# One read for two PSUM banks, double buffers for exponentials, and a new order of work

## The chip, the cores and the metric

The kernel runs on one core of one Trainium2 chip. The metric is the device time of one execution in microseconds (us); the time before is the median of three runs. The profile is one execution, recorded by the hardware profiler. Its engines are PE (TensorE: matmuls), PEld (loads of weights into TensorE), DVE (VectorE), ACT (ScalarE), POOL (GpSimd) and SP (SyncE, which issues all transfers here).

## What is computed

Two branches read the same `x` (2048 tokens of 512) and are mixed by a gate for each token. One is attention with 32 heads of 16 that share one key and one value head, without a mask; the other a gated feed-forward layer of width 1792.

```python
def _A_ref(x, wq, wk, wv, wo):          # B 1, S 2048, D 512, H 32, Dh 16
    q = (x @ wq).reshape(B, S, H, Dh).transpose(0, 2, 1, 3)
    k = x @ wk
    v = x @ wv
    scores = jnp.einsum("bhqd,bkd->bhqk", q, k) * (Dh ** -0.5)
    p = _softmax(scores, axis=-1)
    o = jnp.einsum("bhqk,bkd->bhqd", p, v)
    return o.transpose(0, 2, 1, 3).reshape(B, S, H * Dh) @ wo

def _B_ref(x, w_gate, w_up, w_down):
    g = jnp.einsum("bsd,df->bsf", x, w_gate)
    u = jnp.einsum("bsd,df->bsf", x, w_up)
    return jnp.einsum("bsf,fd->bsd", _sigmoid(g) * u, w_down)

x = A_x
g = _sigmoid((x * gate_w).sum(-1, keepdims=True))
return g * _A_ref(x, A_wq, A_wk, A_wv, A_wo) + (1 - g) * _B_ref(x, B_w_gate, B_w_up, B_w_down)
```

## The kernel before

**Tiling.** Tokens come in 4 blocks of 512 (`NB`, `TB`), keys in 16 chunks of 128 (`NC`). A *unit* is one block of queries for four heads; there are 32 units (`NU`). Matmuls of the feed-forward layer, of the output projections, of the scores and of the maxima use half of the array's rows: the lower lane (h = 0) rows 0 to 63, the upper one (h = 1) rows 64 to 127. The two lanes run at the same time, each into a PSUM bank of its own. Precision is kept by splitting operands into a high and a low part (three products for one), so a projection is a long row of accumulating matmuls.

**The softmax of a unit.** First its maxima: 128 matmuls of queries by keys (line 1092), each into a bank that a reduce on DVE (line 1094) reads at once, 64 for each lane; `max_finish` and `max_turn` fold the partial maxima and SP writes them back into rows of the queries, so that the next matmuls come out less the maximum. Then the scores: 128 matmuls of keys by queries (line 1101), each into a bank that an `Exp` on ACT (line 1103) reads and writes to a buffer `p` in SBUF. Last the values: for each chunk of keys four matmuls over the whole array (line 977; the trace has eight records for them) take the four buffers of that chunk, and sixteen chunks accumulate in one bank. That bank is copied out by ACT (`finish`, line 984) whenever a run of value products ends, since the halves may use other banks next; parts of one unit are added on POOL (line 991). The sums of exponentials take the way over DRAM (`store`, `sums`, `invert`, `send_inverse`, `spread`) and POOL divides by them (`divide`).

**The order.** Nothing is left to a scheduler. `ORDER` is a text, one code for each slot of TensorE, and `plan()` walks it with a clock of its own (`State`). A hexadecimal digit is a slot of two half-array matmuls: the digit divided by 4 says what the lower lane does, the remainder what the upper lane does, 0 nothing, 1 a maximum, 2 a score, 3 a fill (one matmul of a feed-forward or output job). So `5` is a maximum in both lanes, `a` a score in both, `f` a fill in both, `7` a maximum below and a fill above. `V` is a value product, `T` the transpose of maxima, `G` a projection or a transpose of the first stage; these three use the whole array. A `.` is a pause: it moves the clock by 25 units and issues nothing. A slot moves it by 100 units, the change from whole array to halves by 94 (`OUT`) and back by 52 (`IN`).

The clock knows the queues: `on(engine, at, cost)` appends work to an engine. `RED = 260` units is a reduce, `EXP = 208` an exponential, `COPY = 210` a copy; a bank counts as free `TAIL + FREE` units after the computed end of a reduce (38 + 65) and `TAIL_A + FREE_A` after that of an exponential (52 + 60). `take()` gives the bank that has been free longest. `can_s` holds the scores back while all `PB = 21` buffers are in use. Tasks for POOL carry a rank, and an order of SP's transfers follows from the same clock. The result is a list of acts, written out as instructions; at the end of the program every engine is tied to exactly this order. On the chip the clock counts for nothing more: each instruction starts when its engine reaches it and its semaphores allow it.

**The first and the last microseconds.** The first stage (`G`) projects keys, values and queries; `first_x`, `keys_out` and `query_out` keep their tiles in the same ring of `p` buffers. At the end the output projection of the last block has its job in two parts: `a` (three of four head groups; nine fills for each lane and tile) and `e` (unit 30, three fills below only), whose weights `we` are split on POOL (lines 731 and 732) into a ring of four buffers `wd`. The last two heads' share follows from the last bank by transposes (lines 1128 to 1150).

Of the kernel before, what the change touches and what calls it, by code (L numbers as in the profile page):

```python
# [9 lines left out]
F32 = mybir.dt.float32  # L10
F32R = mybir.dt.float32r
AF = mybir.ActivationFunctionType
# [6 lines left out]
P = 128  # L19
# [11 lines left out]
RAW, WB, DB, PB, HB, BA_BUFS = 2, 2, 4, 21, 6, 4  # L31
# [13 lines left out]
EXP, COPY, SCALED = 208, 210, 247  # L45
TAIL, TAIL_A = 38, 52
# [65 lines left out]
class State:  # L112

    def __init__(self):
# [26 lines left out]
        self.held, self.exps = 0, []  # L141
# [329 lines left out]
    def can_s(self, h):  # L471
        j = self.ep[h]
        return (j < NU * NC * 2 and j < self.ep[1 - h] + H_LEAD and self.held < PB
                and self.max_ready.get(j // (2 * NC), NEVER) <= self.now)

    def issue_m(self, h):
        i = self.take()
        self.acts.append(("m", h, self.mp[h], i))
        self.mp[h] += 1
        self.free[i] = self.on("dve", self.now + LATE, RED) + TAIL + FREE  # L480
        if self.mp[h] == min(self.mp) and self.mp[h] % (2 * NC) == 0:
            u = self.mp[h] // (2 * NC) - 1
            self.acts.append(("max_finish", u))
            self.maxima.append((u, self.on("dve", 0, ENDS)))

    def issue_s(self, h):
# [17 lines left out]
    def issue_v(self):  # L504
# [7 lines left out]
        self.held -= 4  # L512
# [106 lines left out]
    def step(self, code):  # L619
# [10 lines left out]
        else:  # L630
# [15 lines left out]
    "GGGGGGG555G55G555.G551G554.G..G55G555G55GG555G55G5ff7ffddff7f5ffffff7fdff7ffdff5G55GTG555G577Gbfed9fedbf6fb7edeb"  # L646
    "7fbd6fdbfef6dbfb7edff55VVVVdaf7f6bdfe7bf9fedb7bed7efedef7bdb7bedff7f55VV555VVV7b7b7bb77bbfdedefedeedfedfedb7bb7b"
    "df6fddd7dVVVTV6ef7f6f9febdf6f9f6fbe7fbdf9e7fe7bf9dbf6ff5dVV695VV696V5bfef6f9fbdef6bdb7ff5dVV5a6.V969V7b6efdfe79f"
    "be7fe7bddd7VVTV5bfedeb7fbde7eb7efdf57VV6ddefbf9fe7bf9fe7b7f5dVVVde6edfb7f9fb7be7dbfe7bdbff6dedbf6fbe7bdfef5VV555"
    "VVV7b7b5bfefededb7ef9fedb7bff6edfed6fbbd7bffd5TVV565VVV5adffeb7fb7edbb7def6febdfe7f9bfdb7ee7edf9f7VV695VVV79fe7b"  # L650
    "def6fef97bfed6fbdbf7edbf9f6feb7dffd75VVa5aVV5a9VV6f7ef97efbd6fbb7efdf5eVV996Vde7bb7efdebde7fe7bdf5bVTV9a5V6de7fb"
    "f9f6fbf6f9fedf5bVV6edfb7f6fbdebdf6fbdf5bVVVV6dfbf67bfedbbdf6fed6fbf6fbdf6bfd9fef6fffb95VV656VV9a5VV5efbf79feb7ef"
    "d9fe7bedff6bfdb7ef9f6fbdb7fed5VTV65aVVVV5bfef97ef9f6febdfe7b7eedf7bbdefdb7be7efd7f6VV959VVV7bdef6dbfe7afdb7f9fed"
    "be7ef7f9bfd6fbf6dfff55VVa5aVTVVVde7bdbe7f9fef6bdbf7edb7bff6debfdb7eed7ef9f7VVde.de7b7bff56VV9dfb7bfedafaVVV6debf"
    "7f9faf9VV76bfede7fdb5VV7b7bbfdedee7e7fed9ff5bVV76bfdef6fbdbdeb7efdf67VV999V67fe7bfedbdeb7f9fe7fd6VTV5a6V5bfededb"
    "fb7ef6f9fdf577VVV97fedbdbfe7ef97bedfb7ee7fdb7befd9feb7fe7fd5VV696VV95aVV7bdef6f9fe79fbedef7e7bdbfedf6fbdaff6dfbf"
    "775VTVVVV97fef9bdf6f9fe7ebfd6feb7dfb7ebfd9feb7fbd7deV569VV65aVVV97fedb7efedb7bf6efde7bdbff6dbfb7edef6dbf7d7VVVVV"
    "9a7ffde7f9fee7dbbdf6fef97bfdbfe7afdfb67ffd6V969VTVa69VV6a6VV9fdbb7edf9fef6f9bf7ffbf7eedf9fe79fee7ff57VV599VVV6f7"
    "bdedbfe7af7debf7f9fffedbb7fed6fbedff75VV596VV9562VV95fefeb7f9faf7f6bfdf5eVV7b79febdfbdee77eedff5bVTV95aV6b7bfdb7"
    "fedef6f9bfde7dVV56aV9b77fedefbdbf6f6dbff6dVV9a5VV6b7ff9def6fbdb7e7ef9fedbfb7debf76fbdefdff55VVVVV6bb7fdfedbe7f6f"  # L660
    "9f6fbed7bff9fed6feb7bdf6ffd9V5a5VTVVV7a7fdebdfb7afd7efb7edbe7ff9f6defb7eedfb7df5VVVa95VVV7a7bfde7fedbbd7bef7eded"
    "bbf7e7fbde7edbbfd7edV5a5VV6b7ff9e7f9fef97ebfde7dVTV6a5Vadf7fbde7bf6f9fe79fd7eVVa95VV6a5Va7fdbf7edb7efbde7bddfaVV"
    "65aV9b7b7fedfe7bdee7fbdd7dVVVV7a7ff9e7fbdef9f6fe7bdbe7dbffe5efbedfb7fef55VVVa95VTVV6b7bfde7f9fef9f6f6f9fee7ff97b"
    "edf9fbf6fdff66VV996VV9a5VV6b7ff97efed6fbdbfb7edbdef7eed7bf9fe7bf7fdd5VVVVV6b7fedbdf6fbbdb7fe7edbef7debdfb7edbfe7"
    "e7f5eV996VTV699VVV7a7fbdf6fbdef9e7fb7bdef6fdbedfe79fbe7fd7ef5VVV977bfefedfa6VV9a9VV5a6V5bfbed7efbf77bb7VdedadedV"
    "V7b7bedfedaf6VV7b7beddefbe5fefb79fef5VV5edeede.f77f9fbbf7bf5faVTV5a6V9b7fdee7fbdaf7edf7fd79VV59aV6b7fdbfedb7af7d"
    "efdf75dVVV7b7bdedef6fbf9f6fbd6fef97efdbfe79fe7bfdff56VV9a5VTVV6b7fdbedf6fef9b7b7fedef97fbdefe79fee7fb7fd5VVV9a5V"
    "VV797bfee7fed9feb7f9fe7ebd7bfe7bdfb7edefedfb6VV965VV965VV97bbf7defe7afdf9ef7e7bdbff6dbf6fedbfe5bfed7TVVV9a5VVV7b"
    "5bb7fefedef6dbef7bdbbdf6f7ef9fede7bf7fde5VV695VV5a6V9b7bfde7fbdee7f9bfde7dVV7a7ff9edf6fe7bbdfee6f7VV959VV9f7eb7d"
    "efedbb7f6efdfedff6fbfb7bbdb7edfef5TVV9a6VV9a5VV6a5V97fbe7edfbdeb7ed7bff5dVV7bb7b7bdfededeb7ffdb77bfbfeedf6feedff"  # L670
    "57ddVVV6a5V977bfef9f6fafddefb75fdVVVV7a7dfbedfeb7be7dfafdb7f6fdefb7eeddbfb7eff95TVVVVV7b5bfee7fedbe7dbefdb7ee7ff"
    "9bdfb76fef9fbdef5V569VVVV6b7fdb7efbdaf7edf6fbdbf6bdf7efed9feb7f5fd7dVVVVV6b7bfde7f9fedeb77bfedbe7ff9efdb7e7ef9fb"
    "d6fdV5a5VV7a7bfde7f9fef9e7f9f7edTVVVVV7a7dfebdfe7bed7bfbdf6fffbedf6f9fe7bbd7fedVVVV7b6fdef9fe7bdbe7fbd6ff77bbVVV"
    "dedeedb7fe7ebddbf6fb7bedbfd7befd6ffee76VV955VTVV9b7fdbedfb7e7edbfedb7edb7eff6dbfbde7bfdff55VVVVV6b7fbdedf6fb7ede"
    "bfdb7ebd7fb7ebfdbdee7fffe65VV995VVV6b7ff9e7fedb7edbe7fedb7bf9fbdf6f6fbf6ffde5dVTVa95VVVV6b7fdeb7f9feed7bf6f9fb7e"
    "feddb7efedb7bfbde7dVV5a5VV6b7ff9edfbe5VV7a7fbdefdbe5VV6b7ff9edfaf5VV6b7bfdfedfa5V7be7fedbbde7f9fe7bdfffef6fb7bbd"
    "edfef67e.f5VV95aV97b7fedbfbde7eede7f7f9VTV95aV6b7bfdbdfe7ede7ebf7df5VVa95VVVV6b5ffbe7f9fe7bdeef79fe7bf9fe7fed9fe"
    "7bffdf66VV9a5VV9a5VV7b7edbf6f9fef9e7edfb7bfe7f97efedbfbd6ffe5f5VVVa95VVTV7b7bdee7f9fedb7bfe7edbf6dbfdee7f9feb7e7"
    "fef5V995VV5a5VVV7a7ff9e7fbde7eedfbdb7bf6edfbde7f6fbbdedf6f7VV995VVV6b7bfde7fbdafd7ef9f6fbdef7ede7bfb7edbff57deVT"
    "Va95VV7a7ff9e7f9fef97edefb7dVV6b7dfeb7f9fee7db7eff9dVVV7a7ff9e7fbdee7dbf9ff6dVV6b7ff9e7fedbf6f9fbdf6dVV6a9VTVVV7"  # L680
    "b79fe7efedaf7edef7dffefbb7bdf9fb7ee7ff9eV5a5VV969V7b7b97fefedee7defb75fdVV5b7bfef9f6feedfbdb7f5dVVVV7a7ff9e7fedb"
    "b7edfed6fbdbfe7edfb79fe7efffb55VVVa95VTVV7a7fdbe7f9febdb7fede7eb7fedb7f9fede7bf6ffd9V5a5VV6a9VVV6b7fdeb7fedbdeb7"
    "fedb7bedbf7dbfe7e7ef9f7d5fdVVVVV7a7bfde7f9fede7bf9f6fbb7dfeedfb7b7edefbd7deV695VV7a7bfdedfb7be7edef79fdVV6a5Vadf"
    "7fb79fef6fbdbd6fd7eVVa95VVTV7a5ffbedf6fbf6bdfe7f9fbfff6dbfedaf7d77fdeVVa95VVVV6b7ff9edf6fbf9b7fed6feb7feddbfe7e7"
    "bdbefffa5VTV595VVV7a7ff9e7fedb7ef9efdb7b7ef9ff6defb7bedfdff65VVa95VVVV6b7bfdedf6fbdeb7fbde7ee7dfbdbfe7b7bedfffe9"
    "5VV695VVV6b7dfebdf6fb7beddefe7bbd7fefb79fe7edefb7f5dVTVa95VVVV6b7fbde7f9fe7bededfb7be7dfe7bdefb7bdefbd6fdVV7b79f"
    "ebdfee5VV5efbe7bdfe7aVV9b7fbdfe7ed5VVV7b7bedefdafaVV6bff6bf9fb7fdef6fefaeVV9b7b7feef9f9ffdef6bfea.VVaaaVVVabbbbb"
    "VVTfeeefafeefbfffffffebaffefbffeVVaaVVVbbfeaVbeaVbaeVafffffbbfffefeeebbVVaefffbbbffeeefVabffffbefeffaVVaaaVVaaaV"
    "Vaa8VV..............Vcccccccccccc"
# [11 lines left out]
def tile_kernel(ctx, tc, x_in, wq, wkv, wo, wg, wu, wd, consts_in, out):  # L701
# [14 lines left out]
    banks = [pp.tile([P, 512], F32, tag=f"bank{i}", name=f"bank{i}") for i in range(8)]  # L716
# [20 lines left out]
    def first_x(b):  # L737

        XR[b] = [ap.tile([P, 512], F32, tag="p", name=f"xf{b}_{kc}", bufs=PB) for kc in range(KC)]
# [158 lines left out]
    def keys_out(b, _, ps):  # L898
        kh = ap.tile([P, TB], F32, tag="p", name=f"kh{b}", bufs=PB).bitcast(F32R)
# [3 lines left out]
        VT[b] = ap.tile([P, TB], F32, tag="p", name=f"vt{b}", bufs=PB)  # L903
# [24 lines left out]
    def query_out(b, t, ps):  # L928
        hi, lo = QD[b, t] = [ap.tile([P, TB], F32R, tag="p", name=f"q{b}_{t}_{i}", bufs=PB) for i in range(2)]
# [270 lines left out]
```

## Time and profile before

| | us |
|---|---|
| three runs | 1599.39, 1599.62, 1601.97 |
| median | 1599.62 |
| the profiled execution | 1598.83 |
| its span, first to last instruction | 1597.1 |

| 40 us from | PE | DVE | ACT |
|---|---|---|---|
| 0 | 37.66 | 28.17 | 18.84 |
| 80 | 40.00 | 38.97 | 27.65 |
| 1540 | 40.00 | 5.23 | 39.91 |

The granted TensorE clock is 1.0 throughout. The page's first lines give busy time and share of the span for each engine. Its costliest groups read: line, engine, operation, output and inputs, shape, count, then busy time and mean ns of one, then idle time of that engine just before them and what ended it. The chain of waits lists start, length and instruction, merged where neighbours are alike. A row of the windows view gives, after its bounds and its length, busy time with the count of instructions for PE, PEld, DVE, ACT and POOL, then the clock, the DMA share and GB/s.

### The profile page before, as it was taken

How to read it: one execution, taken by the hardware profiler on the slowest of the kernel's cores; microseconds unless marked ns; L12 is line 12 of the kernel's file. 1: busy time of each engine (PE TensorE's matmuls, PEld its weight loads, DVE VectorE, ACT ScalarE, POOL GpSimd, SP SyncE). 2: the span in 40 equal slices, each digit the busy share in tenths (PEclk: the TensorE clock that was granted, in tenths of full speed). 3: DMA queues.
4: the chain of work that ended last, by engine and by line, in shares of the span. 5: the costliest groups of instructions: out<-in, count | busy, mean ns of one | idle time of the engine just before them, and what ended most of it. 6: DMA issues, size and time to landing. Idle time of an engine off the chain costs nothing.

```text
span 1597.1 us, 33902 instructions
## 1 busy us (share of the span) xinstructions
PE 1587.9 (99%) x12918; PEld 998.6 (63%) x12918; DVE 1392.0 (87%) x2372; ACT 1258.4 (79%) x2474; POOL 848.0 (53%) x708
## 2 busy tenths in 40 slices
PE   9999999999999999999999999999999999999998
PEld 7776665665656566566666566666656665656654
DVE  7999998998988989988998898889989998988832
ACT  4268778888878878879878877878987887878896
POOL 4254364558363664375745446454936366536463
PEclk9999999999999999999999999999999999999999
DMA  7621121115111212013411121111502021201111
GB/s 239 216 80 42 42 57 36 45 59 137 29 68 32 75 56 60 18 39 83 111 37 58 39 75 54 55 38 59 137 28 68 32 75 46 71 16 42 34 36 44
DMA packets 54678, 102.31 MB, mean 64 GB/s; under 512 B 18232, under 2 KB 19768, under 8 KB 53492
## 3 DMA queue, kind: packets, MB, share of 16 engines
q1 hardware_dynamic: 54516, 100.16, 21.0%
q8 instruction: 101, 1.65, 0.4%
q14 instruction: 61, 0.50, 0.1%
HBM read 74.05 MB, written 13.09 MB: 55 GB/s over the span
## 4 chain that ended last, share of the span: by engine, by line
PE 98%; ACT 0%; DVE 0%; DMA 0%; POOL 0%; issue 0%; DVEq 0%
PE bank L1071 31%; PE bank L977 29%; PE bank L1092 18%; PE bank L1101 16%; PE bank L838 4%; ACT p L1103 0%; PE bank L963 0%; PE bank L908 0%; DVE ba L1148 0%; DVE ba L1034 0%; DMA wkv_raw<-wkv 0%; POOL wkv_s L732 0%; DVE wkv_stack L869 0%; PE bank L1144 0%; DVEq L1196 0%
## 5 line engine op out<-in xcount | busy, mean ns | idle before, releaser
L1094 DVE TENSOR_REDUCE mx<-bank 128x1 f32<-128x512 f32 x2048 | 1257.4, 681 | 133.8 <-PE bank L1092 80.5
L1103 ACT ACTIVATE p<-bank 128x512 f32<-128x512 f32 x2048 | 1050.1, 652 | 2.6 <-PE bank L1101 0.4
L1101 PE MATMUL bank<-qs,ks 64*128 64x512 f32 x2048 | 698.0, 400 | 0.0
L1092 PE MATMUL bank<-ks,qs 62*128 62x512 f32 x2048 | 686.6, 406 | 0.0
L977 PE MATMUL bank<-p,v_aug 128*32 128x512 f32 x4096 | 491.3, 598 | 0.7 <-ACT p L1103 0.7
L1092 PEld LDWEIGHTS bank<-ks,qs 62*128 62x128 f32 x2048 | 338.4, 184 | 151.3 <-issue 51.1
L1101 PEld LDWEIGHTS bank<-qs,ks 64*128 64x128 f32 x2048 | 345.7, 185 | 105.5 <-ACT p L1103 29.9
L991 POOL TENSOR_TENSOR ou<-ou,ou 128x512 f32<-128x512 f32 x201 | 259.0, 1289 | 204.9 <-ACT ou L984 199.2
L984 ACT COPY ou<-bank 128x512 f32<-128x512 f32 x232 | 140.9, 608 | 266.6 <-PE bank L977 122.2
L1071 PE MATMUL bank<-wd,hl 64*128 64x512 f32 x1344 | 273.5, 393 | 0.0
L977 PEld LDWEIGHTS bank<-p,v_aug 128*32 128x32 f32 x4096 | 107.7, 109 | 232.2 <-issue 188.1
L1071 PEld LDWEIGHTS bank<-wd,hl 64*128 64x128 f32 x1344 | 195.0, 185 | 20.4 <-ACT p L1103 1.7
L1071 PE MATMUL bank<-xs,wg 64*128 64x512 f32 x672 | 203.2, 393 | 0.0
L1071 PE MATMUL bank<-xs,wu 64*128 64x512 f32 x672 | 199.7, 393 | 0.0
L1071 PE MATMUL bank<-x,wu 64*128 64x512 f32 x672 | 194.5, 391 | 0.0
L1071 PE MATMUL bank<-x,wg 64*128 64x512 f32 x672 | 190.4, 391 | 0.0
L1071 PEld LDWEIGHTS bank<-xs,wg 64*128 64x128 f32 x672 | 119.7, 185 | 8.1
L1071 PEld LDWEIGHTS bank<-xs,wu 64*128 64x128 f32 x672 | 118.6, 185 | 7.3
L1071 PEld LDWEIGHTS bank<-x,wu 64*128 64x128 f32 x672 | 115.5, 185 | 10.7 <-issue 1.7
L1071 PEld LDWEIGHTS bank<-x,wg 64*128 64x128 f32 x672 | 113.3, 185 | 9.4 <-POOL wu L814 0.8
L1055 POOL TENSOR_TENSOR ba<-ba,pa_d 128x512 f32<-128x512 f32 x48 | 61.8, 1288 | 95.9 <-DVE ba L1034 62.6
L813 POOL CAST wu<-ru 128x1024 fp32r<-128x1024 f32 x27 | 28.1, 1039 | 117.6 <-PE bank L1071 94.3
(83 smaller groups left out, 1064.1 us busy)
## 6 DMA issues: line engine op xcount, KB each, us to landing
rg<-wg SPq DMA_DIRECT2D x28, 512.0 KB
ru<-wu SPq DMA_DIRECT2D x28, 512.0 KB
rd<-wd SPq DMA_DIRECT2D x28, 512.0 KB
qs<-qd SPq DMA_DIRECT2D x192, 64.0 KB
qd<-q SPq DMA_DIRECT2D x32, 256.0 KB
xs<-x SPq DMA_DIRECT2D x16, 512.0 KB
xf<-x_in SPq DMA_DIRECT2D x16, 256.0 KB
ra<-wo SPq DMA_DIRECT2D x8, 512.0 KB
```

Of the source, the lines that this page charges most:

```text
L813: nc.gpsimd.tensor_copy(WS[item][:, 0, :], raw)
L838: nc.tensor.matmul(ps, w[:, p, part(kc)], X[b, kc][:, q, :], start=i == 0, stop=i == 3 * KC - 1)
L977: nc.tensor.matmul(ps[32 * j:32 * j + 32, :], v_aug[:, c, :], PT.pop((u, c, j)), start=start, stop=stop)
L984: nc.scalar.copy(to, ps)
L991: nc.gpsimd.tensor_tensor(SUMS[u], SUMS[u], PARTS_OF[u].pop(0), op=ALU.add)
L1055: nc.gpsimd.tensor_tensor(BA[b, t], BA[b, t], PA.pop((b, t)), op=ALU.add)
L1071: nc.tensor.matmul(banks[i], l, r, start=at == 0, stop=at == j.n - 1)
L1092: nc.tensor.matmul(banks[i], qs_t[u % 3][r, pr, part(qt)], ks[r, kb * 512:(kb + 1) * 512], start=True, stop=True)
L1094: nc.vector.tensor_reduce(MX[u][:, pr, h, qt, kb:kb + 1], banks[i], axis=AX.X, op=ALU.max)
L1101: nc.tensor.matmul(banks[i], ks[r, part(c)], qs_t[u % 3][r, pr, :], start=True, stop=True)
L1103: nc.scalar.activation(p, banks[i], AF.Exp, scale=0.25)
```

## The change

All eight banks become one PSUM tile of eight slices. Where a slot holds a maximum (or a score) in both lanes, both lanes stand at the same count, and two neighbouring banks are free by the planner's clock, the two matmuls go into those banks and one reduce (one exponential) reads both: 1024 columns, two results a row for the maxima. Otherwise the two reads stay apart. `take()` now prefers a bank without a free neighbour. The buffer of an exponential holds both lanes, 2 x 512 columns; there are 10 instead of 21 single ones, and the tiles of the first and last stage that share the ring are paired in the same way. A value product reads halves of two such buffers. `ORDER` is a new text. The planner's costs for the joint reads are `RED_TWO = 488` and `EXP_TWO = 364`.

```diff
-RAW, WB, DB, PB, HB, BA_BUFS = 2, 2, 4, 21, 6, 4
+RAW, WB, DB, PB, HB, BA_BUFS = 2, 2, 4, 10, 6, 4
...
+RED_TWO, EXP_TWO = 488, 364
...
         i = self.free.index(min(self.free))
         assert self.free[i] <= self.now
+        there = [at <= self.now for at in self.free]
+        alone = [n for n in range(8) if there[n] and not any(there[max(n - 1, 0):n] + there[n + 1:n + 2])]
+        if alone:
+            i = min(alone, key=lambda n: self.free[n])
         self.free[i] = NEVER
         return i
+
+    def two_banks(self):
+
+        n = min(range(7), key=lambda n: max(self.free[n:n + 2]))
+        return n if max(self.free[n:n + 2]) <= self.now else None
...
-        return (j < NU * NC * 2 and j < self.ep[1 - h] + H_LEAD and self.held < PB
+        return (j < NU * NC * 2 and j < self.ep[1 - h] + H_LEAD and j - 2 * self.vp < PB
...
+    def issue_mm(self, i):
+        self.acts.append(("mm", self.mp[0], i))
+        self.mp = [n + 1 for n in self.mp]
+        self.free[i:i + 2] = [self.on("dve", self.now + LATE, RED_TWO) + TAIL + FREE] * 2
+        self.unit_maxima(0)
...
+    def issue_ss(self, i):
+        self.acts.append(("ss", self.ep[0], i))
+        e = self.ep[0] // 2 - self.vp
+        self.ep = [n + 1 for n in self.ep]
+        at = self.on("act", self.now + LATE_A, EXP_TWO) + TAIL_A
+        self.free[i:i + 2] = [at + FREE_A] * 2
+        self.exp_done(e, 2, at)
...
-            for h, what in enumerate(divmod(int(code, 16), 4)):
+            two = {"5": self.mp, "a": self.ep}.get(code)
+            two = self.two_banks() if two and two[0] == two[1] else None
+            if two is not None:
+                self.done += 100
+                (self.issue_mm if code == "5" else self.issue_ss)(two)
+            for h, what in enumerate(divmod(int(code, 16), 4) if two is None else ()):
...
-    banks = [pp.tile([P, 512], F32, tag=f"bank{i}", name=f"bank{i}") for i in range(8)]
+    both = pp.tile([P, 8, 512], F32, tag="banks", name="banks")
+    banks = [both[:, i, :] for i in range(8)]
...
-            nc.tensor.matmul(ps[32 * j:32 * j + 32, :], v_aug[:, c, :], PT.pop((u, c, j)), start=start, stop=stop)
+            nc.tensor.matmul(ps[32 * j:32 * j + 32, :], v_aug[:, c, :], PT[u, c, j // 2][:, j % 2, :], start=start, stop=stop)
...
+    def two_maxima(n, i):
+        for h in range(2):
+            to = keys_by(h, n, i + h)
+        nc.vector.tensor_reduce(to, both[:, i:i + 2, :], axis=AX.X, op=ALU.max)
...
+        if (u, c, pr) not in PT:
+            PT[u, c, pr] = ap.tile([P, 2, 512], F32, tag="p", name=f"p{u}_{c}_{pr}", bufs=PB)
+        return PT[u, c, pr]
...
+    def two_scores(n, i):
+        for h in range(2):
+            p = by_keys(h, n, i + h)
+        nc.scalar.activation(p, both[:, i:i + 2, :], AF.Exp, scale=0.25)
```

The two texts, first and last lines:

```diff
 ORDER = (
-    "GGGGGGG555G55G555.G551G554.G..G55G555G55GG555G55G5ff7ffddff7f5ffffff7fdff7ffdff5G55GTG555G577Gbfed9fedbf6fb7edeb"
...
-    "VVTfeeefafeefbfffffffebaffefbffeVVaaVVVbbfeaVbeaVbaeVafffffbbfffefeeebbVVaefffbbbffeeefVabffffbefeffaVVaaaVVaaaV"
-    "Vaa8VV..............Vcccccccccccc"
+    "GGGGGGG555G55G55.5G551....4G55GG555G55GG555G55G555GG57ffffd5ffff5fffff7ffff5fff7fdffdf7fdf7dff7fTG55Gafdbfef7adb"
...
+    "affffafffffbfefbeffaeVVaaaVVVVbaffffaffaffVVc.......................................cccccccccccc"
 )
```

More of the change, by code (lines that the diff above doesn't have):

```diff
@@ L480, in issue_m, with unit_maxima @@
         self.free[i] = self.on("dve", self.now + LATE, RED) + TAIL + FREE
+        self.unit_maxima(h)
+    def issue_mm(self, i):
[3 more added lines that the diff above has]
+        self.unit_maxima(0)
+    def unit_maxima(self, h):
         if self.mp[h] == min(self.mp) and self.mp[h] % (2 * NC) == 0:
@@ L651 @@
[L651 to L665, printed above, removed]
@@ L690 @@
+    "e7fedb7edb7bfedbf7ed7VVV5efbdbfb6fe6VV6deff9fb79faVV9edfe77bffaaVV5bfe7bfedfaaVV9edf7eb7fedee7f97bffbaVVaaaVVVV7"
+    "b7b7bfedbd9fbbdff7fe7efb7bfedededee7fedbV6aaVTVaaaVVVfafafafffffaffffaa.VVaaaVVaa2.aVVVbaaffffffaffeaVVbaaVaffff"
+    "affafffffbfefbeffaeVVaaaVVVVbaffffaffaffVVc.......................................cccccccccccc"
 )
@@ L737, in first_x @@
     def first_x(b):
-        XR[b] = [ap.tile([P, 512], F32, tag="p", name=f"xf{b}_{kc}", bufs=PB) for kc in range(KC)]
+        two = [ap.tile([P, 2, 512], F32, tag="p", name=f"xf{b}_{i}", bufs=PB) for i in range(KC // 2)]
+        XR[b] = [two[kc // 2][:, kc % 2, :] for kc in range(KC)]
         for kc in range(KC):
@@ L898, in keys_out @@
     def keys_out(b, _, ps):
-        kh = ap.tile([P, TB], F32, tag="p", name=f"kh{b}", bufs=PB).bitcast(F32R)
+        two = ap.tile([P, 2, TB], F32, tag="p", name=f"kh{b}", bufs=PB)
+        kh = two[:, 0, :].bitcast(F32R)
         nc.scalar.activation(kh, ps, AF.Identity, bias=rows[:, 1:2])
@@ L902, in keys_out @@
                                        op0=ALU.mult, op1=ALU.add)
-        VT[b] = ap.tile([P, TB], F32, tag="p", name=f"vt{b}", bufs=PB)
+        VT[b] = two[:, 1, :]
         nc.scalar.copy(VT[b], ps)
@@ L928, in query_out @@
     def query_out(b, t, ps):
-        hi, lo = QD[b, t] = [ap.tile([P, TB], F32R, tag="p", name=f"q{b}_{t}_{i}", bufs=PB) for i in range(2)]
+        two = ap.tile([P, 2, TB], F32R, tag="p", name=f"q{b}_{t}", bufs=PB)
+        hi, lo = QD[b, t] = two[:, 0, :], two[:, 1, :]
         nc.scalar.copy(hi, ps)
@@ L1085, in h_split, with keys_by @@
         HS[b, f] = split(HS[b, f], hl, nc.gpsimd.tensor_copy, nc.gpsimd)
-    def maximum(h, n, i):
+    def keys_by(h, n, i):
         s, pr = divmod(n, 2)
@@ L1093, in maximum, with by_keys @@
                          start=True, stop=True)
-        nc.vector.tensor_reduce(MX[u][:, pr, h, qt, kb:kb + 1], banks[i], axis=AX.X, op=ALU.max)
-    def scores(h, n, i):
+        return MX[u][:, pr, :, qt, kb]
+    def maximum(h, n, i):
+        to = keys_by(h, n, i)
+        nc.vector.tensor_reduce(to[:, h:h + 1], banks[i], axis=AX.X, op=ALU.max)
+    def two_maxima(n, i):
+        for h in range(2):
+            to = keys_by(h, n, i + h)
+        nc.vector.tensor_reduce(to, both[:, i:i + 2, :], axis=AX.X, op=ALU.max)
+    def by_keys(h, n, i):
         e, pr = divmod(n, 2)
@@ L1101, in scores @@
         nc.tensor.matmul(banks[i], ks[r, part(c)], qs_t[u % 3][r, pr, :], start=True, stop=True)
-        p = PT[u, c, 2 * pr + h] = ap.tile([P, 512], F32, tag="p", name=f"p{u}_{c}_{pr}_{h}", bufs=PB)
-        nc.scalar.activation(p, banks[i], AF.Exp, scale=0.25)
+        if (u, c, pr) not in PT:
+            PT[u, c, pr] = ap.tile([P, 2, 512], F32, tag="p", name=f"p{u}_{c}_{pr}", bufs=PB)
+        return PT[u, c, pr]
+    def scores(h, n, i):
+        p = by_keys(h, n, i)
+        nc.scalar.activation(p[:, h, :], banks[i], AF.Exp, scale=0.25)
+    def two_scores(n, i):
+        for h in range(2):
+            p = by_keys(h, n, i + h)
+        nc.scalar.activation(p, both[:, i:i + 2, :], AF.Exp, scale=0.25)
     on_bank = lambda act: lambda *args: act(*args[:-1], banks[args[-1]])
@@ L1111, in tile_kernel @@
         "f": fill, "gate": gate, "gated": gated, "h": h_split, "part": part_of, "add": add_part, "out": send_out,
-        "m": maximum, "max_finish": max_finish, "max_turn": on_bank(max_turn), "send_max": send_max, "s": scores,
+        "m": maximum, "max_finish": max_finish, "max_turn": on_bank(max_turn), "send_max": send_max, "s": scores, "mm": two_maxima, "ss": two_scores,
         "values": on_bank(pv), "finish": on_bank(finish), "store": store, "sums": sums, "invert": invert, "send_inverse": send_inverse,
@@ L1122, in tile_kernel @@
     n0 = (NB - 1) * NT
-    spare = lambda name: ap.tile([P, TB], F32, tag="p", name=name, bufs=PB)
+    spare = lambda name: ap.tile([P, 2, TB], F32, tag="p", name=name, bufs=PB)[:, 0, :]
     end, rest = banks[end], [bank for i, bank in enumerate(banks) if i != end]
```

74 lines of the change are left out of this document (44 added, 30 removed).

## Prediction

> **What bounds the kernel now.** I read the page first (busy times, chain by engine, costliest groups), then the chain of waits in order of time, then the end.
>
> ```profile
> PE 1587.9 (99%) x12918; PEld 998.6 (63%) x12918; DVE 1392.0 (87%) x2372; ACT 1258.4 (79%) x2474; POOL 848.0 (53%) x708
> PE 98%; ACT 0%; DVE 0%; DMA 0%; POOL 0%; issue 0%; DVEq 0%
> L1094 DVE TENSOR_REDUCE mx<-bank 128x1 f32<-128x512 f32 x2048 | 1257.4, 681 | 133.8 <-PE bank L1092 80.5
> L1103 ACT ACTIVATE p<-bank 128x512 f32<-128x512 f32 x2048 | 1050.1, 652 | 2.6 <-PE bank L1101 0.4
> L977 PE MATMUL bank<-p,v_aug 128*32 128x512 f32 x4096 | 491.3, 598 | 0.7 <-ACT p L1103 0.7
> ```
>
> TensorE is busy for 99% of the span and carries 98% of the chain that ended last. "Busy" alone would not prove that it never stalls, since ends of matmuls are modelled; but the page gives its value products (L977) 0.7 us of idle time in all. So a faster read on VectorE or ScalarE shortens nothing directly. What can change the time is what TensorE is asked to do, and whether it begins to wait for banks. Its price list comes from the chain in order of time; x16 of L977 are two value products.
>
> ```profile
> 274.76 3.57 PE bank L977 x32
> 288.53 1.85 PE bank L977 x16
> 291.29 1.85 PE bank L977 x16
> 294.04 1.85 PE bank L977 x16
> ```
>
> A value product costs (3.57 - 1.85) / 2 = 0.86 us. Between 278.33 and 288.53 the order has 43 slots (10.20 us); between 290.38 and 291.29 it has three (0.91 us). So one slot costs (10.20 - 0.91) / 40 = 0.232 us. From 288.53 to 291.29 pass 2.76 us for two value products (1.72), three slots (0.70) and one change from whole array to halves and back: 0.34 us. The prices fit with nothing over, so slots follow each other without stalls.
>
> **Part 1, the new order.** Counted in the two texts of ORDER: both hold 4258 slots, 512 V, 32 T, 24 G; 4404 fills, 2048 maxima, 2048 scores. The number of matmuls is the same. But neighbouring codes change between whole array (V, T, G) and halves 477 times before and 449 times after: 28 changes less, 14 pairs, 14 x 0.34 = **4.7 us less** (three of the 14 stand among the projections; I price them alike). Two of the 24 G move behind the first V, and with each its two stores of q on SP; they are the last queries of the last block, which only the last quarter of the units reads, and SP and the transfers have room. Taken as 0.
>
> Pauses ("."): 23 before, 84 after. A pause is no instruction; it moves the planner's clock by 25 units, and since 100 units are one slot it stands for 0.058 us. TensorE waits there only where a semaphore really makes it. Before, 14 stand ahead of the last V, and the end shows what they are (first line from the chain, the others from the timeline):
>
> ```profile
> 1575.80 7.95 ACT p L1103 x16
> 1583.80 1.06 PE L977 MATMUL bank<-p,v_aug 128*32 128x512 f32 x8 [0.70 <-ACT p L1103]
> 1576.75 0.60 POOL L731 CAST we<-re 64x512 fp32r<-64x512 f32 x1
> 1577.43 1.28 POOL L732 TENSOR_TENSOR we<-re,we 64x512 fp32r<-64x512 f32 x1
> ```
>
> There TensorE waits 0.70 us for exponentials. In the new text those pauses are gone: **0.7 us less**. Instead 39 pauses (2.3 us) stand between the last c of the attention output and the twelve c of the last two heads. The planner lets the split of `we` start only when that whole output group has ended; its buffer is one of four, last read in the first third of the last job, with six more fills and two V before the end. POOL needs 0.60 + 1.28 = 1.9 us for the split, and those fills and V last about 2 x 0.86 + 5 x 0.232 + 0.34 = 3.2 us. So most of it is covered; bounds 0 and 2.3, I take **+0.3**. Of the other 45 pauses (9 before), 36 more x 0.058 = 2.1 us is the upper bound, 0 the lower. The planner frees a bank 112 units (TAIL_A + FREE_A, 0.26 us) after an exponential's computed end, while above TensorE starts 0.05 us after it (7.95 from 1575.80 ends at 1583.75, the start is at 1583.80). 0.21 us of margin is more than a pause: **+0.3**.
>
> **Part 2, maxima of both lanes in one reduce.** No group of before reads two banks. The bounds for the second 512 columns, from the groups by shape and, in the last line, the timeline:
>
> ```profile
> L956 DVE TENSOR_REDUCE mm<-mx 128x16 f32<-128x64 f32 x32 | 7.0, 220 | 1.1
> L1128 ACT COPY ou_last<-bank 128x256 f32<-128x256 f32 x2 | 0.6, 375 | 1.2 <-PE bank L977 1.2
> L1141 ACT COPY o_last<-bank 128x128 f32<-128x128 f32 x2 | 0.5, 265 | 4.3 <-PE bank L1139 4.3
> L804 ACT CAST wg<-rg 128x1024 fp32r<-128x1024 f32 x1 | 1.1, 1050 | 0.0
> L769 ACT CAST x<-rx 128x1024 fp32r<-128x1024 f32 x6 | 6.2, 1121 | 0.0
> L756 ACT CAST x<-xf 128x512 fp32r<-128x512 f32 x16 | 9.1, 621 | 5.4 <-DMA xf<-x_in 3.3 <-PE bank L838 2.0
> 1553.42 7.46 ACT L1103 ACTIVATE p<-bank 128x512 f32<-128x512 f32 x15
> ```
>
> Reduce: 681 - 220 over 448 columns is 1.03 ns each, 0.53 us for 512. At 1257.4 / 2048 = 0.61 us apiece a pair took 1.23 and takes 1.14 us. The planner counts RED_TWO = 488 units = 1.13 us: it agrees. At most 282 pairs (the codes 5) save VectorE up to 25 us. VectorE is not on the chain, so **0**; without that cover the order would still be the one written out, so nothing is gained either.
>
> **Part 3, scores of both lanes in one exponential.** Alone, an exponential follows the last at (7.46 - 0.61) / 14 = 0.49 us. The second 512 columns cost 0.44 (265 to 375 over 128 columns, 0.86 ns each), 0.43 (621 to 1050) or 0.50 us (621 to 1121). I take 0.43, the pair 0.92 against 0.98 for two. ScalarE saves up to 259 x 0.06 = 16 us: off the chain, **0**.
>
> The Trainium skill, "ScalarE: Activation LUTs", section "What ACT_TABLE_LOAD costs", gives 0.833 ns per column whatever the function; by it the second bank is 0.427 us, and the sum at the end would be some 0.7 us lower. The trace agrees, with 0.43 and 0.44.
>
> But the order was laid out with EXP_TWO = 364 units, 0.85 us at 0.232 per 100. (EXP = 208 units is 0.48: right.) So **each double exponential ends 0.07 us later than the order assumes**, and so does what is queued behind it on ScalarE until the engine idles, with no instruction added: other exponentials, gate tanh, scaled copies. TensorE waits for the banks of all of them. ScalarE idles where it waits for a run of V to end:
>
> ```profile
> L984 ACT COPY ou<-bank 128x512 f32<-128x512 f32 x232 | 140.9, 608 | 266.6 <-PE bank L977 122.2
> 1540.00:1580.00 40.00, 40.00 (x331) 20.60 (x323) 5.23 (x9) 39.91 (x81) 23.72 (x22) 1.00 0.08 18
> ```
>
> 1.15 us idle per copy: the lag starts again at nought with nearly every run of V. Up to the last maximum the text has 226 codes a: 111 stretches between whole-array codes hold one, 30 two, 13 three, 4 four. Of the 0.21 us of margin I take 0.13 as free on the mean, the upper half, because of that idle time. Then one or two cost nothing, three 0.21 - 0.13 = 0.08, four 0.15: 13 x 0.08 + 4 x 0.15 = **+1.6 us**. Bounds: 0.3 (all 0.21 free: only fours pay, 4 x 0.07) and 226 x 0.07 = 15.8 (no margin). After the last maximum 33 codes a follow, in a stretch like the one from 1540 to 1580, where ScalarE (fourth number, 39.91 of 40) never idles and the lag adds up: 33 x 0.07 - 0.13 = **+2.2**, bounds 0 and 2.3.
>
> **Part 4, 10 double buffers for 21 single ones, one PSUM tile for eight.** Exponentials idled 2.6 us in all (L1103), so no buffer was short; half a double less, and a double stays taken until both halves are read. The loads of x and the stores of q keep their number on SP. Taken as 0; below by 0, above by those 2.6 us once more.
>
> **Sum** on the profiled execution: span 1597.1 - 4.7 - 0.7 + 0.3 + 0.3 + 1.6 + 2.2 = 1596.1; outside the span lie 1598.83 - 1597.1 = 1.7: **1597.8 us**. The profiled execution was 0.8 below the median 1599.62; I leave that in, it is within the spread 1599.39 to 1601.97. This is 0.1% faster, which I call no change: about 0.2%, 3.2 us, is what a measurement of this kernel can tell.
>
> **Rivals.** (a) *No lag reaches TensorE*: the double read runs in the assumed 0.85, or the margin swallows it. For: exponentials are 208 units in the planner and in the trace. Against: every row gives 0.43 or more for 512 columns. 1597.1 - 5.4 + 0.3 + 1.7 = 1593.7, faster by 0.3%.
> (b) *ScalarE sets the pace, slower.* The place is each stretch with an a between runs of V; the price 0.07 a piece, with no margin because a double keeps its first bank 0.43 us longer (0.92 for 0.49) while the second comes only 0.06 sooner, so that the order runs short of neighbouring banks, as its 36 further pauses say. All of it gives 1597.1 - 5.4 + 15.8 + 2.3 + 0.6 + 1.7 = 1612.1. It decides from 9.4 us of stalls in all: 1597.1 - 5.4 + 9.4 + 1.7 = 1602.8, 3.2 over the median; beside the end and the pauses that is 6.6 of the 15.8. Against: the idle 266.6 us. The Trainium skill, "PSUM — Partial Sum Buffer", section "Summary: rules for kernel authors", says to empty banks promptly, which speaks against holding one for its neighbour; by that rule the time would be this rival's, and no run here has shown it yet.
> (c) *The pairs don't come about*: a code 5 or a falls back to two single reads if no two neighbouring banks are free. Then no read lags: 1593.4 to 1594. Against: the codes 5 grow from 215 to 282 and the codes a from 137 to 259.
> (d) *One tile for eight banks makes reads wait for other banks' matmuls.* Each of 2048 exponentials in series with its matmul would add 2048 x 0.49 = 1000 us. Nothing in the trace speaks for it, the slices of the one tile being disjoint.
>
> **Numbers.** Forecast 0.50 (own range 1594.5 to 1602; 0.10 of it faster, 0.38 same, 0.02 slower), (a) 0.23, (c) 0.04, (b) 0.20, (d) 0.03. Faster 0.37, same 0.38, slower 0.25. The range goes down to 1593, just below (a) and (c), and up to 1605, a third into (b).
>
> **What would show it.** Right: the chain has some 14 changes less and its slot stays 0.232; double exponentials follow at 0.92 and double reduces at 1.14; TensorE's idle time behind ScalarE is some 4 us, half of it after 1540. Wrong: doubles at 0.85 and no such waits (a); such waits all along (b); few doubles (c). A time under 1593 would mean that I missed a gain, one over 1605 that the lag adds up over stretches.

## The result and the profile after

The changed kernel takes **1609.71 us** (median of 4 runs, 1609.07 to 1610.92) against 1599.51 us before (1599.28 to 1601.97). The ratio is 1.0061, 95% interval 1.0044 to 1.0079: **slower by 0.6%**, 10.2 us. The profiled execution took 1609.33 us, its span is 1607.5 us, and the granted clock is 1.0 in both. The forecast of 1597.8 us was wrong, and so was its range up to 1605.

The page of the changed kernel, its lines for the engines, the chain by engine and the groups that answer to those of before (L1156 and L1161 are the single and the double exponential, L1137 and L1142 the single and the double reduce, L1016 the value product, L1023 the copy behind a run of V):

```profile
PE 1597.7 (99%) x12918; PEld 996.8 (62%) x12918; DVE 1388.1 (86%) x2203; ACT 1239.9 (77%) x2233; POOL 837.6 (52%) x699
PE 97%; DVE 1%; ACT 1%; DMA 0%; SPq 0%; issue 0%; DVEq 0%; ACTq 0%
...
L1137 DVE TENSOR_REDUCE mx<-banks 128x1 f32<-128x512 f32 x1710 | 1059.7, 682 | 117.2 <-PE banks L1131 85.5
L1156 ACT ACTIVATE p<-banks 128x512 f32<-128x512 f32 x1584 | 816.8, 652 | 6.0 <-PE banks L1149 3.0
...
L1016 PE MATMUL banks<-p,v_aug 128*32 128x512 f32 x4096 | 489.7, 598 | 0.3 <-ACT p L1161 0.3
...
L1023 ACT COPY ou<-banks 128x512 f32<-128x512 f32 x223 | 132.8, 596 | 281.5 <-PE banks L1016 178.2
...
L1161 ACT ACTIVATE p<-banks 128x1024 f32<-128x1024 f32 x232 | 238.2, 1046 | 4.9 <-PE banks L1149 0.2
L1142 DVE TENSOR_REDUCE mx<-banks 128x2 f32<-128x1024 f32 x169 | 203.6, 1219 | 30.5 <-PE banks L1131 28.3
```

Both double reads come about: 232 exponentials (of 259 codes a) and 169 reduces (of 282 codes 5). ScalarE and VectorE are less busy than before (1239.9 against 1258.4 us, 1388.1 against 1392.0), with 241 and 169 instructions fewer. TensorE runs the same 12918 matmuls, and its busy time has grown by 9.8 us (1597.7 against 1587.9), which is nearly the whole loss. The page shows no waiting: the value products idle 0.3 us, and TensorE still carries 97% of the chain. The loss is hidden inside "busy": a half-array matmul is on record for 0.39 us or more while slots follow each other at 0.232, so a slot that comes 0.1 us late leaves no gap.

It shows where stretches of equal length are laid side by side. This is the chain of the changed kernel in order of time; between 476.36 and 486.80 its order has 43 slots, as many as the stretch priced in the prediction.

```profile
471.93 4.43 PE banks L1016 x40
...
478.18 0.25 PE banks L1110 x3
478.43 0.30 PE banks L1131
478.74 0.23 PE banks L1149 x2
...
480.35 0.32 PE banks L1131 x2
...
485.82 0.28 PE banks L1131
...
486.80 1.00 PE banks L1016 x8
```

The 43 slots of the stretch before took 10.20 us, these take 10.44. Nearly all slots of the list still take 0.23 us, but the pieces at 478.43, 480.35 and 485.82 take 0.07, 0.09 and 0.05 more: 0.21 of the 0.24 us. All three begin with a matmul for maxima (L1131).

One such place close up. The first fence is the timeline of ScalarE, the next that of TensorE's weight loads (in brackets the idle time before, and who ended it), the third that of its matmuls:

```profile
553.52 1.10 ACT L1161 ACTIVATE p<-banks 128x1024 f32<-128x1024 f32 x1
```

```profile
553.90 0.47 PEld L1110 LDWEIGHTS banks<-wd,hl 64*128 64x128 f32 x4
554.67 0.19 PEld L1131 LDWEIGHTS banks<-ks,qs 62*128 62x128 f32 x2 [0.29 <-ACT p L1161]
554.77 0.19 PEld L1149 LDWEIGHTS banks<-qs,ks 64*128 64x128 f32 x1
```

```profile
554.13 0.67 PE L1110 MATMUL banks<-wd,hl 64*128 64x512 f32 x4
554.67 0.50 PE L1131 MATMUL banks<-ks,qs 62*128 62x512 f32 x2
555.01 0.40 PE L1149 MATMUL banks<-qs,ks 64*128 64x512 f32 x1
```

The double exponential ends at 554.62 and frees two banks; the two matmuls for maxima start in them at 554.67, 0.02 and 0.07 us late in their lanes. But their weight loads could not run ahead as those of L1110 did: they start at 554.67 too, the two matmuls last 0.50 us where the next one lasts 0.40, and the load of the next slot (L1149) starts only at 554.77. So the next slot starts 0.34 us later instead of 0.232. **A bank that comes free just in time costs the slot behind it 0.1 us, because the weight load waits with its matmul and is no longer hidden.**

How often that happens can be counted by setting each refill of a bank beside the end of the read that freed it; the "lead" is the time from that end to the start of the matmul. For neighbouring slots without V or pause between them, this is what the next slot takes beyond 0.2325 us, worked out from the starts and ends in the four traces (the last two columns are experiments told below):

```
lead             before          after           after, short     before, short
under 100 ns     5:   0.3 us    72:   4.9 us    14:   1.2 us      4:   0.3 us
100 to 150 ns   50:   0.8      224:   3.7       44:   1.0        11:   0.2
more, or none 3708:  -0.4     3462:   1.6     3700:  -0.1      3748:  -1.3
```

In the changed kernel the mean price is 81 ns under 66 ns of lead, 65 to 80 ns, 52 to 100, 30 to 120, 13 to 150, and 2 beyond. In all, slots take 0.6 us beyond 0.2325 each before, and 10.2 after.

The rest of the difference lies in the start: up to the first V the changed kernel is 2.0 us behind its order's own clock (0.1 ahead before). VectorE's reduces are on the chain there once, and so is one transfer.

```profile
22.23 2.31 DMA qs<-qd
...
33.54 3.41 DVE mx L1142 x3
```

The transfer is on the chain of this execution only; in the profile of the control below it isn't, and the lag up to the first V is 1.6 us.

### The profile page after: what moved, and what is told of

Same layout as the page of the kernel before. It is cut to its first block, busy times and chain, and to the rows that moved or that the text cites. A ratio compares the mean times of both kernels' runs of the same rounds, so it can differ in the third digit from the quotient of the medians.

```text
span 1607.5 us, 33550 instructions
## 1 busy us (share of the span) xinstructions
PE 1597.7 (99%) x12918; PEld 996.8 (62%) x12918; DVE 1388.1 (86%) x2203; ACT 1239.9 (77%) x2233; POOL 837.6 (52%) x699
## 4 chain that ended last, share of the span: by engine, by line
PE 97%; DVE 1%; ACT 1%; DMA 0%; SPq 0%; issue 0%; DVEq 0%; ACTq 0%
PE banks L1110 31%; PE banks L1016 29%; PE banks L1131 18%; PE banks L1149 15%; PE banks L875 2%; PE banks L1002 0%; DMA wqr<-wq 0%; DVE ba L1073 0%; SPq L990 0%; DVE mx L1142 0%; ACT p L1161 0%; DMA qs<-qd 0%; DVE ba L1206 0%; ACT x L793 0%; DVE q L970 0%
## 5 line engine op out<-in xcount | busy, mean ns | idle before, releaser
L1137 DVE TENSOR_REDUCE mx<-banks 128x1 f32<-128x512 f32 x1710 | 1059.7, 682 | 117.2 <-PE banks L1131 85.5
L1156 ACT ACTIVATE p<-banks 128x512 f32<-128x512 f32 x1584 | 816.8, 652 | 6.0 <-PE banks L1149 3.0
L1131 PE MATMUL banks<-ks,qs 62*128 62x512 f32 x2048 | 682.9, 414 | 0.8 <-DMA qs<-qd 0.6
L1149 PE MATMUL banks<-qs,ks 64*128 64x512 f32 x2048 | 672.7, 398 | 0.6 <-DVE ba L1073 0.5
L1016 PE MATMUL banks<-p,v_aug 128*32 128x512 f32 x4096 | 489.7, 598 | 0.3 <-ACT p L1161 0.3
L1131 PEld LDWEIGHTS banks<-ks,qs 62*128 62x128 f32 x2048 | 330.3, 184 | 171.1 <-issue 41.4
L1149 PEld LDWEIGHTS banks<-qs,ks 64*128 64x128 f32 x2048 | 330.0, 185 | 73.2 <-ACT p L1161 18.0
L1023 ACT COPY ou<-banks 128x512 f32<-128x512 f32 x223 | 132.8, 596 | 281.5 <-PE banks L1016 178.2
L1110 PE MATMUL banks<-wd,hl 64*128 64x512 f32 x1344 | 271.0, 394 | 0.0
L1016 PEld LDWEIGHTS banks<-p,v_aug 128*32 128x32 f32 x4096 | 108.3, 109 | 231.6 <-issue 189.7
L1161 ACT ACTIVATE p<-banks 128x1024 f32<-128x1024 f32 x232 | 238.2, 1046 | 4.9 <-PE banks L1149 0.2
L1142 DVE TENSOR_REDUCE mx<-banks 128x2 f32<-128x1024 f32 x169 | 203.6, 1219 | 30.5 <-PE banks L1131 28.3
L1110 PEld LDWEIGHTS banks<-wd,hl 64*128 64x128 f32 x1344 | 190.1, 185 | 31.6 <-issue 3.4
L1110 PE MATMUL banks<-x,wu 64*128 64x512 f32 x672 | 199.5, 394 | 0.0
L1110 PE MATMUL banks<-xs,wg 64*128 64x512 f32 x672 | 197.2, 393 | 0.0
L1110 PE MATMUL banks<-xs,wu 64*128 64x512 f32 x672 | 197.0, 393 | 0.0
L1110 PE MATMUL banks<-x,wg 64*128 64x512 f32 x672 | 193.5, 393 | 0.0
L1110 PEld LDWEIGHTS banks<-x,wu 64*128 64x128 f32 x672 | 114.9, 185 | 16.3 <-issue 5.9
L1110 PEld LDWEIGHTS banks<-x,wg 64*128 64x128 f32 x672 | 112.6, 185 | 16.5 <-POOL hl L767 4.2
L1110 PEld LDWEIGHTS banks<-xs,wg 64*128 64x128 f32 x672 | 114.9, 185 | 6.8 <-issue 0.8
L1110 PEld LDWEIGHTS banks<-xs,wu 64*128 64x128 f32 x672 | 114.7, 185 | 5.8
```

What stands on the lines that cost most here:

```text
L1016: nc.tensor.matmul(ps[32 * j:32 * j + 32, :], v_aug[:, c, :], PT[u, c, j // 2][:, j % 2, :], start=start, stop=stop)
L1023: nc.scalar.copy(to, ps)
L1110: nc.tensor.matmul(banks[i], l, r, start=at == 0, stop=at == j.n - 1)
L1131: nc.tensor.matmul(banks[i], qs_t[u % 3][r, pr, part(qt)], ks[r, kb * 512:(kb + 1) * 512], start=True, stop=True)
L1137: nc.vector.tensor_reduce(to[:, h:h + 1], banks[i], axis=AX.X, op=ALU.max)
L1142: nc.vector.tensor_reduce(to, both[:, i:i + 2, :], axis=AX.X, op=ALU.max)
```

## The experiments

Four theories are told apart. **A, lag**: double exponentials end later than the order counts on, and TensorE waits for their banks. **B, holding**: a double read keeps its first bank until the second is done. **C, order only**: the new sequence is slower whatever the reads do. **D, closeness**: the new order takes banks so soon after their computed release that any read late by some 0.1 us costs a slot, a single one too. In the shared runs the kernel before took 1600.3 to 1600.4 us.

**Both double reads split.** The order, the banks and the buffers stay; each double read becomes two single ones.

```diff
-        nc.vector.tensor_reduce(to, both[:, i:i + 2, :], axis=AX.X, op=ALU.max)
+        for h in range(2):
+            nc.vector.tensor_reduce(to[:, h:h + 1], banks[i + h], axis=AX.X, op=ALU.max)
...
-        nc.scalar.activation(p, both[:, i:i + 2, :], AF.Exp, scale=0.25)
+        for h in range(2):
+            nc.scalar.activation(p[:, h, :], banks[i + h], AF.Exp, scale=0.25)
```

> The changed kernel with its order, banks and buffers, but every joint read is made as two reads one after the other. Theory A (lag): the order counts a joint exponential as 0.85 us; joint it takes 0.91, apart 0.97, so the second bank and all that is queued behind it on ScalarE come 0.12 instead of 0.06 late: slower than the changed kernel, 1612 to 1622 us. Theory B (holding): banks suffer because the first waits for the end of both reads; apart it is free 0.4 earlier: 1598 to 1602. Theory C (the order itself is too tight, whatever reads): 1609 +- 2.

Measured 1618.27 us, ratio 1.0115 (1.0100 to 1.0130). The split frees the first bank of each pair earlier and is 8.6 us slower than the changed kernel: B is out as the main cause, and C too. The double reads help within this order; split, they take more time on ScalarE, of which the order has too little.

**Only the exponentials split** (the second half of that diff).

> Only the joint exponentials are made apart, the joint reduces stay. A: as with both apart, since VectorE's joint reduce takes what the order counts: 1612 to 1622, within 3 us of both apart. B: between the changed kernel and both apart, 1600 to 1606. C: 1609 +- 2.

1617.03 us, ratio 1.0105 (1.0088 to 1.0122): 7.3 of the 8.6 us come from ScalarE.

**Only the reduces split** (the first half).

> The changed kernel, only the joint reduces are made apart. Lag theory: a joint reduce takes 1.13 us as the order counts, two take 1.20, so the second bank comes 0.06 us late, on VectorE this time and at 169 places: 2 to 5 us slower than the changed kernel, 1611 to 1615. If holding the first bank were the harm: faster, 1605 to 1608.

1611.20 us, ratio 1.0067 (1.0052 to 1.0082): 1.5 us more than the changed kernel in the median. The two intervals overlap; between the first V and the last maximum its trace is 0.8 us longer, so the split costs some 1 us. VectorE has more room than ScalarE, as A says, and again nothing is won by releasing the first bank early.

**A control for shorter exponentials.** The next kernels compute fewer columns, so the value products must not read the rest: here they read the first 256 columns of each tile twice, and the exponentials stay whole.

```diff
-            nc.tensor.matmul(ps[32 * j:32 * j + 32, :], v_aug[:, c, :], PT[u, c, j // 2][:, j % 2, :], start=start, stop=stop)
+            nc.tensor.matmul(ps[32 * j:32 * j + 32, :], v_aug[:, c, :], PT[u, c, j // 2][:, j % 2, :256].unsqueeze(1).to_broadcast([P, 2, 256]), start=start, stop=stop)
```

> The changed kernel, but value products read the first 256 columns of an exponential twice in place of 512 different ones (so the result of attention is left out for half of the queries). Control for the next one. All theories: as the changed kernel, 1609.5 +- 1.5.

1609.61 us, ratio 1.0061 (1.0046 to 1.0076): the changed operand costs nothing.

**Double exponentials as short as the order counts them**: 475 columns of each bank.

```diff
-        nc.scalar.activation(p, both[:, i:i + 2, :], AF.Exp, scale=0.25)
+        nc.scalar.activation(p[:, :, :475], both[:, i:i + 2, :475], AF.Exp, scale=0.25)
```

> The control, and each joint exponential computes 475 of the 512 columns of each bank (the rest is left out): 950 columns, 74 less x 0.83 ns = 0.06 us shorter, 0.85 as the order counts. A: the lag is gone, 1597 to 1600. B: banks are held nearly as long, 1606 to 1609. C: 1609 +- 2.

1603.87 us, ratio 1.0020 (1.0010 to 1.0029). Taking away 0.07 us (1046 ns to 980 in the mean) from 232 instructions on an engine that is busy for 77% wins 5.7 us. That is A's direction but not its size: 3.5 us of the loss are left though the doubles now run as counted. This miss led to D.

**Shorter still**: 438 columns, less than the order counts.

> As the control with short joint exponentials, but 438 of 512 columns of each bank (the rest is left out): 0.79 us, 0.06 less than the order counts. After the 475-column run some 4 us over the kernel before were left. Theory D (closeness): the new order takes a bank within 25 units of its computed end 608 times, the old one 323 times, so the usual scatter of ScalarE's ends costs more; then 0.06 earlier at 232 places and behind them saves another 2 to 3 us, 1600.5 to 1602. If the rest is in the first stage, the pauses or the buffers: 1603 to 1604 as with 475.

1601.36 us, ratio 1.0007 (0.9998 to 1.0017). Another 2.5 us: reads that are early by the order's count still win time, as D says and A does not.

**All exponentials short**: the doubles 438 columns, the singles 464.

> As before, and the single exponentials compute 464 of 512 columns, 0.04 us less each (the rest is left out): no end on ScalarE is late any more. Theory D: only stalls behind VectorE (some 1.9 us in the trace of the 475-column run) and the first stage stay, 1598 to 1600.5. Otherwise 1602 to 1604.

1597.56 us, ratio 0.9982 (0.9972 to 0.9992), lower than D gave. The singles were as right in the order as before, and shortening them wins 3.8 us. Shorter exponentials thus win this order 1609.6 - 1597.6 = 12.0 us. The stretch from above, in the chain of this kernel:

```profile
470.10 4.43 PE banks L1016 x40
...
476.59 0.22 PE banks L1131
...
484.76 1.00 PE banks L1016 x8
```

From 474.53 to 484.76 the same 43 slots take 10.23 us, and the piece that took 0.30 takes 0.22. The weight loads that waited behind exponentials (us in total, times, longest) show the same; of the changed kernel, of the one with all exponentials short, and of the kernel before:

```profile
PEld banks L1131 <- ACT p L1161: 33.5, 80, 0.8
PEld banks L1131 <- ACT p L1156: 28.6, 73, 0.8
PEld banks L1149 <- ACT p L1161: 18.0, 45, 0.8
PEld banks L1149 <- ACT p L1156: 11.4, 42, 0.8
```

```profile
PEld banks L1131 <- ACT p L1161: 20.1, 24, 0.8
PEld banks L1131 <- ACT p L1156: 13.6, 17, 0.8
PEld banks L1149 <- ACT p L1161: 12.8, 16, 0.8
...
PEld banks L1149 <- ACT p L1156: 4.2, 5, 0.8
```

```profile
PEld bank L1092 <- ACT p L1103: 30.1, 47, 0.8
PEld bank L1101 <- ACT p L1103: 29.9, 53, 0.8
```

The count is what tells, not the sum, for most of a load's waiting lies beside running matmuls: 240 loads for maxima and scores waited in the changed kernel, 62 with short exponentials, 100 before.

**The old order with a lag put into it.** The kernel before, with a copy of 8 columns on ScalarE behind every 14th exponential of each lane.

```diff
+    idle = cp.tile([P, 16], F32, name="idle")
+    nc.gpsimd.memset(idle, 0.0)
...
+        if n % 14 == 0:
+            nc.scalar.copy(idle[:, :8], idle[:, 8:])
```

> The kernel before, its order and buffers untouched, with a copy of 8 columns on ScalarE behind every 14th exponential of each lane (some 146 copies of about 0.1 us, 14 us in all, as much as 232 x 0.06). Lag theory: banks come late here as well, 3 to 9 us slower than before. If lag costs nothing where all reads are single: no change, within 1 us.

1607.99 us, ratio 1.0048 (1.0033 to 1.0063). This group of ScalarE is the addition:

```profile
L1107 ACT COPY idle<-idle 128x8 f32<-128x8 f32 x148 | 36.4, 246 | 0.0
```

Busy time counts 246 ns for one, most of it beside its neighbours: from the end of one exponential to the end of the next pass 0.58 us with a copy between them and 0.49 without (medians), so a copy takes 0.09 us, some 13 us in all. TensorE loses 7.7 us to them, though ScalarE's busy share stays at 79%. So an unforeseen 0.09 us in ScalarE's queue costs the old order, too, more than half of itself; this needs no double read and no new order.

**The old order with short exponentials**, the counterpart of the kernel with all exponentials short: 464 columns, and value products as in the control.

> The kernel before, with its exponentials computing 464 of 512 columns of each bank and the value products reading the first 256 columns of each tile twice (so that part of the scores is left out). It is the counterpart of the changed kernel with all its exponentials shortened, which took 1597.6 us. Theory (only an order that is late loses): the old order loses about 0.8 us behind late single exponentials, so shortening them saves 0.3 to 1.5 us: 1598.0 to 1599.3, beside 1599.5 for the kernel before; the new order without lag is then 0.5 to 2 us better than the old one without lag. Rival (every exponential, late or not, costs the old order as much as it does the new one): 1596 to 1597.5, and the new order is worth nothing even without lag.

1597.51 us, ratio 0.9985 (0.9976 to 0.9994). The theory missed: the old order wins 2.8 us, not 0.3 to 1.5. So without lag the two orders stand at 1597.5 and 1597.6 us, and the rival's second half is right: **the new order is worth nothing that can be measured even where nothing in ScalarE is late.** Its first half is not, since shortening wins the new order 12.0 us.

## Why the prediction was wrong

The outcome is rival (b), the one on the other side: ScalarE's lag reaches TensorE all along. The time lies between the rival's least, 1602.8, and its most, 1612.1, and its 15.8 us for the body are nearer to the 11.2 found below than the 1.6 of the sum. Half of its reason was wrong: banks held for their neighbour are not the main cause, as the split reads show, so the sentence in the Trainium skill, "PSUM — Partial Sum Buffer", section "Summary: rules for kernel authors", to empty banks promptly, led here to the right side by a way that these runs don't bear out.

**Part 1, the new order: -4.7, -0.7, +0.3, +0.3.** A pair of changes between whole array and halves takes 0.34 to 0.36 us in the mean in all four traces of the table of leads, as priced, and the pauses behave as argued: 36 stand between slots now and 3 before, and such a slot takes 0.245 us in the mean, beside 0.235 for a plain one of that kernel, 0.4 us in all. The 39 at the end cost nothing. In the chain at the end TensorE runs through them without a piece of another engine up to 1595.6:

```profile
1590.86 0.93 PE banks L1110 x8
...
1593.18 1.97 PE banks L1016 x16
1595.15 0.44 PE banks L1110
```

POOL had split `we` by 1590.0, as this row of its timeline says, well before it was needed:

```profile
1588.76 1.28 POOL L768 TENSOR_TENSOR we<-re,we 64x512 fp32r<-64x512 f32 x1
```

Yet the sum of these terms, -4.8 us, does not appear between the two orders without lag. Two places in those two traces give back most of it. By the table of leads, with exponentials short, slots take 2.1 us beyond 0.2325 each in the new order (1.2 + 1.0 - 0.1) and 0.8 us less in the old (0.3 + 0.2 - 1.3): 2.9 us. Of these, 1.5 stand behind late banks that VectorE frees, which under 150 ns of lead cost 1.8 us against 0.3. And up to the first V the new order is 1.0 us further behind its own clock. For the last microsecond or so no single place was found.

**Part 2, reduces of two banks: 0.** The duration was right. The timeline of VectorE has three in a row:

```profile
33.46 3.48 DVE L1142 TENSOR_REDUCE mx<-banks 128x2 f32<-128x1024 f32 x3
```

(3.48 - 1.22) / 2 = 1.13 us each, with 1.22 as the mean of one. "Nothing is gained either" was short by what the split cost, some 1 us.

**Part 3, exponentials of two banks.** The duration was right as well; here four stand in a row on ScalarE behind an idle time:

```profile
1557.32 0.59 ACT L1023 COPY ou<-banks 128x512 f32<-128x512 f32 x1 [0.25 <-PE banks L1016]
1557.93 3.77 ACT L1161 ACTIVATE p<-banks 128x1024 f32<-128x1024 f32 x4
```

(3.77 - 1.05) / 3 = 0.91 us, forecast 0.92, counted by the order 0.85. The Trainium skill, "ScalarE: Activation LUTs", section "What ACT_TABLE_LOAD costs", with 0.833 ns a column, again agrees with the second bank's 0.91 - 0.49 = 0.42 us. The "some 0.7 us" that the prediction would take off the sum by that figure are 0.3 by its own terms: a lag of 0.067 in place of 0.07 gives 1.47 + 2.08 where it had 1.64 + 2.18.

**The step that failed is the margin**: "Of the 0.21 us of margin I take 0.13 as free on the mean, the upper half, because of that idle time. Then one or two cost nothing." The lag term of +1.6 us in the body was mis-sized: it measured 11.2 us. Setting each stretch of the changed kernel up to the last maximum beside the same stretch with all exponentials short, by the starts of its value products:

```
codes a in the stretch     stretches   longer by, us   each
none, over five slots          24          0.85        0.035
one, over five slots           51          5.71        0.112
two, over five slots           24          2.46        0.103
three, over five slots         11          1.13        0.102
four, over five slots           3          0.43        0.143
any number, to five slots      88          0.57        0.006
```

A long stretch with one pays 0.11 us, and one with three no more; but single exponentials are short here too. Beside the 475-column run, where only the doubles change, to the length that the order counts, a long stretch of the changed kernel is longer by 0.005 us with none, 0.034 with one, 0.049 with two, 0.069 with three and 0.12 with four: with the short stretches 4.9 us in all. So the doubles' own lag does start again behind each run of V and does grow with their number, as the prediction had it, and three and four cost about the 0.08 and 0.15 that it gave them; but ones and twos, put at nothing, cost 2.9 us together. The other 6.3 of the 11.2 us remain when every exponential takes what the order counts, and the sum had no term for them.

The margin was misread in three ways. The 0.21 us was taken to the start of the matmul, while the table of leads shows that a bank must be free some 0.15 us before, so that the weight load can go ahead. The planner's 0.26 us run from an end computed by the spacing of exponentials, while the end in the trace comes 0.11 us later (0.60 us for one alone, 0.49 spaced). Where a bank freed by an exponential is taken within 25 units of its computed release, the matmul starts 0.19 us after that end in the mean in the kernel before (229 banks), but 0.14 us behind singles and 0.12 behind doubles in the changed one (434 banks): 0.04 us was free before, and nothing is now. And a margin is a mean: exponentials scatter, and in the new order single ones at their right price are among the late as well (183 of the 296 leads under 150 ns are theirs, 76 those of doubles). Where the prediction looked at ScalarE's idle 1.15 us per run of V, it should have looked at how many banks are taken close to their release. In the planner's own times 618 banks are taken within 25 units (0.06 us) of their computed release in the new order, and 343 in the old (the expectation of the 438-column run had 608 and 323). Taking banks strictly in the order in which they come free, whatever their neighbours, would leave 588 in the new one, so it is the sequence that is tight and not the choice of neighbouring banks.

By stages, against the orders' own clocks (2.3256 ns a unit, 0.2326 us a slot), the four kernels stand as follows. In the profiles of the two short ones nine of the first projections take 3.72 us, where they take 2.33 in the other two, so that all behind them starts some 2 us later; that lies in their first row.

```
behind the order's clock, us     before   after   after, short   before, short
at the first V                     -0.1     2.0        3.2            2.2
first V to last maximum             4.6    15.8        4.6            2.9
last maximum to last V              0.1     0.8       -0.4           -0.9
```

The lag in the body is 15.8 - 4.6 = 11.2 us, within the bounds of 0.3 to 15.8 but far from 1.6, and the old order had 4.6 - 2.9 = 1.7 us of it. After the last maximum it is 0.8 + 0.4 = 1.2 against the +2.2 forecast; the old order had 0.1 + 0.9 = 1.0 there.

**Part 4, buffers and the one PSUM tile: 0.** The exponentials idle 6.0 + 4.9 us in all against 2.6; that is off the chain. Rival (d) is out: nothing is in series.

Rival (a) needed doubles at 0.85 us, and run so they still lose 3.5 us. Rival (c) is out by the counts.

What stays open: an order laid out with 0.91 us for a double exponential and a later release of banks was not tried on the chip. No kernel of this study beats the kernel before with the whole computation in it.

## What to carry to other kernels

In a sequence that was laid out by computed times, a row with a duration is not enough: ask how long before its use each buffer is due, and price a read that ends late by what its neighbour in TensorE's queue loses, from the first one on. A margin counts only beyond what the weight load needs ahead of its matmul, and the mean idle time of the reading engine is no part of it. When TensorE's busy time grows while its instructions stay the same, lay equal stretches of the chain side by side: the waits are inside "busy".

## What the runs showed of the hardware

A bank freed less than 0.15 us before the matmul that refills it cost the next slot 13 to 81 ns in the mean and up to 108 ns at worst, although the matmul itself started little late (0.02 and 0.07 us at 554.67); the trace showed its weight load starting with it, not ahead of it. A copy of 8 columns from SBUF to SBUF between two exponentials kept ScalarE's queue 0.09 us, though it is on record for 0.246, and 148 of them made a kernel whose ScalarE is busy for 79% of the time 7.7 us longer.
